# Polysketch attention and ELU experts on one core: batch 2's x from products of 64 rows, and a new order of the calls up to group 6

## The chip, the cores and the metric

The kernel runs on one core of one Trainium2 chip. The metric is device time in microseconds (us); less is better. A core has five engines that work side by side, each in the order of its own queue: TensorE (PE in the profile; its weight loads are PEld), VectorE (DVE), ScalarE (ACT), GpSimd (POOL) and SyncE (SP), which in this kernel only issues transfers. TensorE writes into PSUM, a memory of eight banks; the other engines read it from there. All other tiles lie in SBUF, a memory of 128 partitions.

## The reference

The program computes an attention block and feeds its output to an expert block with the ELU activation.

```python
# B, H, S, D = 4, 4, 1088, 32;  r = 8;  all float32
def phi(x):                       # 8 x 8 = 64 features
    a = einsum('rd,bhsd->bhsr', S1, x)
    b = einsum('rd,bhsd->bhsr', S2, x)
    return einsum('bhsi,bhsj->bhsij', a, b).reshape(B, H, S, 64)
q_p, k_p = phi(q), phi(k)
kv  = einsum('bhsf,bhsd->bhfd', k_p, v)      # 64 x 32 per head
z   = sum(k_p, axis=2)
num = einsum('bhsf,bhfd->bhsd', q_p, kv)
den = einsum('bhsf,bhf->bhs', q_p, z)[..., None] + 1e-6
x   = (num / den).transpose(0, 2, 1, 3).reshape(4352, 128)
h   = x @ w_in                               # 128 x 2048
g   = where(h > 0, h, exp(min(h, 0)) - 1)
out = g @ w_out                              # 2048 x 128
```

## The kernel before

**Tiles.** The 4352 tokens are cut into groups g = 0 to 8. Groups 0 and 1 are batch 0, 2 and 3 batch 1, 4 and 5 batch 2, 6 and 7 batch 3, each of 512 tokens; group 8 has the 64 tokens that are left over of each batch. The hidden width of 2048 is cut into eight pairs `cp` of 2 x 128 rows. One (g, cp) is called a step of the expert block here, and goes through the engines thus:

- `mm1(g, cp)` (line 910), TensorE: h = W_in x, two halves of 128 x 512, each into a PSUM bank of its own; four banks carry the tag "h" and are used in turn.
- `elu_a` (line 923), ScalarE: relu(-h) on line 930 and the exponential on line 932, giving e; `elu_d` (line 934), VectorE: gg = max(e - 1, h) on line 938. After it the bank is free for the next tenant.
- `sums7` (line 791), GpSimd: three sums of quarters of gg. `mm2_seven` (line 819), TensorE: W_out gg as seven products of half size (Strassen's way), which needs these sums. Group 0, and the first pair of group 1, use plain products instead (`mm2`, `mm2_blocks`).
- At the end of a group `fin_seven_copy`, `fin_seven_a`, `fin_seven_b` (lines 843 to 889; ScalarE, then VectorE) put the seven products together from the two banks "o0" and "o1", and `fin_seven_c` (line 890) transposes the result on VectorE and issues 16 stores on SP's queue (line 901).

**The queries.** The x of a group comes from its query features and the kv of its batch. `queries(g5s, g1s, step)` (line 751) takes two of the h banks, under the name of a step of the expert block, and two of the tag "aux". It makes two kinds of products into them: for groups in `g1s` the sketches of the queries (`q1`, line 567; products of 32 rows), for groups in `g5s` x itself. Between the two, VectorE makes the query features of a group: `q1_out` (copies to SBUF), `q2_prod`, `q2_sum`, `q2_rec`, `q2_an` (the denominator and the division by it), `q2_half` (the outer product, in two halves i; `q2_a` puts one factor into PSUM first), and `q4(g, i)` (line 702), which turns them so that the features lie on partitions.

x is made in one of two ways, by the tuple `pairs` on line 330. A group that isn't in it takes `q5` (line 719): the 64 features are summed in two products of 32 rows, f = 0 and 1, and `q4` is one VectorE transpose (line 707). A group in `pairs` takes `q5_pairs` (line 731): one product of 64 rows. For this the two feature halves of a head must lie in neighbouring blocks of 32 partitions, and `q4` has to move them there: a VectorE transpose (line 711), then eight transfers between partitions on SP's queue (line 717) for each half i, from the tile qpF to the tile raw or qpE. An entry g of `pairs` covers g and g + 1, as one `queries` call does. Before, these are groups 6 and 7 (batch 3) and group 8; groups 2, 3 (batch 1) and 4, 5 (batch 2) take `q5`.

**kv.** `KA(b)` (line 446) makes kv of batch b on TensorE. `KT_out(b)` (line 458) transposes it, stores it in DRAM (line 462, SP) and reads it back in the form that the products need, also on SP: four loads into `kvs[b]` (line 465) for `q5`, four or two loads into `kv2[b]` (line 469) for `q5_pairs`.

**Batch 0** starts the kernel and has helpers of its own (`KF_first`, `KO_first`, `KA_first`, `q1_first`, `q4_early`, `q5_early`, `den_turn`, `den_out` and others); its x comes from `q5_early_out` (lines 670 to 679) and starts the expert block through `mm1_first`. `q4_early` transposes query features on TensorE, four transposes a call. `transp` (line 284) transposes q or k on VectorE.

**Weights.** w_in and w_out arrive as 64-bit floats in words of 32 bits. `R1(f, i)` runs one of the steps strip, floor, shift, round_s, low, whole (lines 117 to 145) on one slice i of them; they are spread over VectorE, ScalarE and GpSimd in the first 40 us. `weights7` sums quarters of W_out for `mm2_seven`.

**The order.** From line 1022 to line 1893 the calls stand in an order written out by hand: what is called first goes first into the queue of its engine, and the semaphores follow from the data and from the reuse of buffers. From `steps[32]` (group 6, pair 0) on, a loop (lines 1896 to 1921) issues the steps in turn. `width[0] = 64` (line 1622) lets the products of `mm1` and `mm2_seven` that are issued after it go in tiles of 64 columns.

Of the kernel before, what the change touches and what calls it, by code (L numbers as in the profile page):

```python
# [12 lines left out]
F32 = mybir.dt.float32  # L13
# [16 lines left out]
def kernel(  # L30
# [301 lines left out]
    pairs = (6, 8)  # L332
    pair_b = [g // 2 for g in pairs if g < 8]
    kvs = {b: const.tile([P, H, 2, D], F32, name=f"kvs{b}") for b in (1, 2)}
# [141 lines left out]
    def Z(b, ps, zl):  # L476

        quarters(ps[:, 96:128], SXh[:], zl[:], None if b else 64)
# [547 lines left out]
    KF_first((0, 1), (4, 0))  # L1026
    KF_first((1, 1))
    KF_first((2, 1))
    transp(kT, "k", 0, 5, KT)
    KF_first((5, 0), (3, 1))  # L1030
    KF_first((6, 0), (4, 1))
    KF_first_out(0)
    transp(kT, "k", 0, KT + 5, NT)
# [3 lines left out]
    KF_first_out(1)  # L1037
    KF_first_out(2, slice(1, 2))
    KF_first_out(2, slice(0, 1))
    transp(qT, "q", 0, 0, 8)  # L1040
    KO_first(5, 6)
    Z_first(0, 1, 2)
    q1_first(0, 1)
    Z_first(3, 4, 5)
    Z_first(6, 7, 8)
    q1_first(2, 3)
    KO_first(3, 5)
    KO_first(6, 9)
    make_Sxp()
    KO_pool(0, 3)  # L1050
    load_rest()
    zl = ZC(0, feats["z"])
    Z(0, feats["z"], zl)
    Z_out(0, feats["z"])
    q1_first_out()
    KA_first(range(0, 5), True, False)
    zq = q1z_first()
    q2_out(0, 0)
    q2_out(0, 1)
    transp(qT, "q", 0, 8, 13)  # L1060
    q4_early(0, 0)
    KA_first(range(5, 9), False, True)
    q4_early(0, 1)
    q2_prod(0, zq)
    R1(strip, 0, nc.scalar)
    R1(low, 0)
    R1(strip, 1, nc.scalar)
    q4_out(0, 0)
    transp(qT, "q", 0, 13, NT)
    abwp = q1_second()  # L1070
    q2_sum(0)
    R1(floor, 0)
    KS_copy()
    KS_turn()
    q2_rec(0)
    den_wide()
# [4 lines left out]
    R1(shift, 0)  # L1081
    R1(shift, 1)
    q4_out(0, 1)
    R1(strip, 2, nc.scalar)
    den_out()
    R1(round_s, 1)
    q5_early(0)
    q2_prod(1)
    R1(low, 1, nc.gpsimd)
    R1(round_s, 0)  # L1090
    whole_half(0, 0)
    q2_sum(1)
    q5_early_out(0, 0)
    R1(low, 2)
    R1(low, 3)
    R1(low, 4)
    R1(strip, 3, nc.scalar)
    q5_early_out(0, 1)
    mm1_first(0, (0,))
    mm1_first(0, (1,))  # L1100
    elu_a(0, 0, 0, (0,))
    R1(strip, 4)
    q2_rec(1)
    R1(floor, 4)
    q2_an(1)
    R1(shift, 4)
    whole_half(0, 1)
    R1(whole, 1)
    mm1_first(1, (0, 1))
    elu_a(0, 0, 0, (1,))  # L1110
    q2_out(1, 1)
    mm1(0, 1, (1,))
    mm1(0, 1, (0,))
    q4_early(1, 1)
    R1(round_s, 4)
    q2_out(1, 0)
    elu_d(0, 0, 0)
    elu_a(0, 0, 1, (0,))
    q4_early(1, 0)
    elu_a(0, 0, 1, (1,))  # L1120
    elu_a(0, 1, 1, (0,))
    elu_a(0, 1, 1, (1,))
    elu_d(0, 0, 1)
    R1(whole, 4)
    mm1(0, 2, (0,))
    mm1(0, 2, (1,))
    R1(floor, 2)
    R1(shift, 2)
    R1(round_s, 2)
    q4_out(1, 1)  # L1130
    q4_out(1, 0)
    R1(strip, 7)
    elu_d(0, 1, 1)
    KT_out(0)
    elu_a(0, 1, 0, (0,))
    R1(floor, 3)
    R1(strip, 5)
    R1(whole, 2)
    elu_a(0, 2, 1, (0,))
    elu_a(0, 1, 0, (1,))  # L1140
    q5_early(1)
    q5_early_out(1, 1)
    q5_early_out(1, 0)
    mm2(0, 0, False, (0,))
    R1(shift, 3)
    R1(floor, 5)
    R1(low, 5)
    R1(round_s, 3)
    elu_a(0, 2, 1, (1,))
    R1(shift, 5)  # L1150
    R1(whole, 3)
    weights7(slice(1, 2), 0)
    mm2(0, 0, False, (1,))
    elu_a(0, 2, 0, (0,))
    elu_a(0, 2, 0, (1,))
    elu_d(0, 1, 0)
    R1(floor, 7)
    mm1(1, 0, (1,))
    mm1(1, 1, (0,))
    elu_d(0, 2, 1)  # L1160
    mm1(1, 0, (0,))
    R1(round_s, 5)
    elu_a(1, 1, 0, (0,))
    elu_a(1, 1, 0, (1,))
    R1(strip, 6)
    elu_d(0, 2, 0)
    R1(strip, 8)
    R1(floor, 6)
    R1(shift, 6)
    R1(floor, 8)  # L1170
    R1(round_s, 6)
    R1(whole, 5)
    elu_a(1, 0, 0, (0,))
    elu_a(1, 0, 0, (1,))
    R1(low, 6)
    elu_a(1, 0, 1, (0,))
    R1(shift, 7)
    mm2(0, 1, False, (0,))
    elu_a(1, 0, 1, (1,))
    R1(low, 7)  # L1180
    elu_d(1, 0, 0)
    mm2(0, 1, False, (1,))
    mm2(0, 2, False, (0,))
    mm2(0, 2, False, (1,))
    transp(kT, "k", 1, 9, NT)
    R1(shift, 8)
    R1(round_s, 7)
    mm1(1, 1, (1,))
    elu_a(1, 1, 1, (0,))
    elu_a(1, 1, 1, (1,))  # L1190
    R1(low, 8)
    transp(kT, "k", 1, 0, 9)
    elu_d(1, 0, 1)
    R1(whole, 6)
    mm2_blocks(0, (0,))
    mm1(0, 3, (0,))
    R1(low, 9)
    elu_d(1, 1, 1)
    R1(strip, 9)
    elu_d(1, 1, 0)  # L1200
    KF_late(1, None)
    R1(strip, 10)
    R1(round_s, 8)
    elu_a(0, 3, 0, (0,))
    elu_a(0, 3, 0, (1,))
    elu_d(0, 3, 0)
    R1(whole, 7)
    mm1(0, 3, (1,))
    elu_a(0, 3, 1, (0,))
    mm1(0, 4, (1,))  # L1210
    mm2_blocks(0, (1,))
    elu_a(0, 3, 1, (1,))
    mm1(0, 4, (0,))
    elu_a(0, 4, 0, (0,))
    elu_d(0, 3, 1)
    elu_a(0, 4, 0, (1,))
    KF_late_out(1, 1)
    weights7(slice(2, 4), 0)
    make_SWs()
    R1(floor, 10)  # L1220
    R1(floor, 9)
    R1(shift, 10)
    elu_d(0, 4, 0)
    R1(shift, 9)
    transp(kT, "k", 2, 0, 9)
    R1(round_s, 9)
    mm2(0, 3, False, (0,))
    mm2(0, 3, False, (1,))
    R1(whole, 8)
    mm1(0, 5, (0,))  # L1230
    mm1(1, 2, (1,))
    mm1(0, 5, (1,))
    R1(whole, 9)
    elu_a(0, 4, 1, (0,))
    elu_a(0, 4, 1, (1,))
    elu_d(0, 4, 1)
    KF_late_out(1, 0)
    elu_a(0, 5, 0, (0,))
    KO(1, 0, nc.gpsimd)
    mm2(0, 4, False, (0,))  # L1240
    mm2(0, 4, False, (1,))
    elu_a(0, 5, 1, (0,))
    elu_a(0, 5, 1, (1,))
    elu_d(0, 5, 1)
    elu_a(0, 5, 0, (1,))
    elu_d(0, 5, 0)
    KO_a(1, 1)
    KO_b(1, 1)
    R1(round_s, 10)
    transp(qT, "q", 1, 0, 9)  # L1250
    mm1(0, 6, (0,))
    R1(low, 10)
    R1(whole, 10)
    elu_a(0, 6, 0, (0,))
    mm1(1, 2, (0,))
    mm2(0, 5, False, (0,))
    elu_a(0, 6, 0, (1,))
    elu_a(1, 2, 1, (0,))
    elu_a(1, 2, 1, (1,))
    elu_a(1, 2, 0, (0,))  # L1260
    elu_a(1, 2, 0, (1,))
    KA(1, (0,))
    weights7(slice(1, 2), 1)
    KA(1, (1,))
    mm1(0, 6, (1,))
    transp(qT, "q", 1, 9, NT)
    KT_out(1)
    elu_d(0, 6, 0)
    weights7(slice(0, 1), 2)
    weights7(slice(2, 4), 1)  # L1270
    mm2(0, 5, False, (1,))
    zls[1] = ZC(1, kv_ps[1])
    sums7(1, 1, 0)
    Z(1, kv_ps[1], zls[1])
    elu_a(0, 6, 1, (0,))
    elu_a(0, 6, 1, (1,))
    elu_d(1, 2, 1)
    Z_out(1, kv_ps[1])
    Z_share(1)
    elu_d(0, 6, 1)  # L1280
    elu_d(1, 2, 0)
    sums7(1, 2, 0)
    weights7(slice(1, 2), 2)
    mm1(0, 7, (0,))
    elu_a(0, 7, 0, (0,))
    elu_a(0, 7, 0, (1,))
    mm2(0, 6, False, (0,))
    mm2(0, 6, False, (1,))
    mm1(0, 7, (1,))
    transp(kT, "k", 3, 0, 9)  # L1290
    elu_a(0, 7, 1, (0,))
    elu_d(0, 7, 0)
    sums7(1, 1, 1)
    weights7(slice(0, 1), 0)
    weights7(slice(1, 2), 3)
    sums7(1, 1, 2)
    transp(kT, "k", 3, 9, NT)
    queries((), (2,), (1, 4))
    mm1(1, 3, (0,))
    q1_out(2, (2,))  # L1300
    mm2(0, 7, True, (0,))
    q1_out(2, (1,))
    weights7(slice(4, 8), 0)
    elu_a(0, 7, 1, (1,))
    elu_d(0, 7, 1)
    q1_out(2, (3,))
    mm2(0, 7, True, (1,))
    mm1(1, 4, (1,))
    q1_out(2, (0,))
    q2_prod(2)  # L1310
    elu_a(1, 3, 0, (0,))
    elu_a(1, 3, 0, (1,))
    mm1(1, 3, (1,))
    elu_a(1, 3, 1, (0,))
    elu_d(1, 3, 0)
    fin1(0)
    q2_sum(2)
    sums7(1, 2, 1)
    weights7(slice(4, 8), 2)
    q2_rec(2)  # L1320
    elu_a(1, 4, 1, (0,))
    q2_an(2)
    mm1(1, 6, (1,))
    mm1(1, 4, (0,))
    elu_a(1, 3, 1, (1,))
# [648 lines left out]
```

## Time and profile before

| What | Value |
|---|---|
| median of 3 runs | 260.21 us (259.96 to 260.28) |
| the profiled execution, its own time | 260.24 us |
| its span | 258.3 us |
| granted TensorE clock, mean | 1.00 |
| longest busy on other engines: GpSimd, ScalarE, VectorE | 183.9, 182.1, 175.6 us |

The page gives one profiled execution. "Busy" is the time in which an engine executes, the percentage its share of the span. The page's table of the costliest groups shows which work this is and how the engines wait:

```profile
L938 DVE SCALAR_TENSOR_TENSOR gg<-e,h 128x512 f32<-128x512 f32 x128 | 85.4, 683 | 59.7 <-ACT e L932 42.2
L259 PE MATMUL h<-xg,W 128*32 128x512 f32 (+2 forms) x768 | 121.5, 584 | 0.7 <-DVE xg L678 0.7
L930 ACT ACTIVATE e<-h 128x512 f32<-128x512 f32 x128 | 75.0, 591 | 52.4 <-PE h L259 50.4
L795 POOL TENSOR_TENSOR tt<-gg 128x512 f32<-128x512 f32 x55 | 71.6, 1301 | 26.6 <-DVE gg L938 21.1
```

A row reads: line, engine, operation, the tile written and the tiles read, count; busy time in us and mean ns of one; then the idle time of the engine just before these instructions, and what ended most of it. ScalarE idles 52.4 us in front of line 930, and TensorE's h ends 50.4 us of that: ScalarE waits for TensorE.

### The profile page before, as it was taken

Reading aid. Unit: us, or ns where it says so; the run is one execution under the profiler, and the core shown is the slowest. Engines: PE = TensorE matmul, PEld = TensorE weight load, DVE = VectorE, ACT = ScalarE, POOL = GpSimd, SP = SyncE. Lnnn points to the kernel's source line nnn. Section 1 sums busy time; section 2 is a strip of 40 time slices with the busy share of each in tenths; the row PEclk is TensorE's granted clock in tenths of the full one; section 3 lists DMA queues with packets and bytes.
Section 4 is the critical chain, followed back from the end, with each engine's and each line's share of the span. In section 5 each row is a group of like instructions: output and inputs, shape, how many; then the busy total and the mean of one; then the engine's idle time right before and its main releaser. Section 6 shows DMA issues by size and latency. Waiting matters only on the chain.

```text
span 258.3 us, 9815 instructions
## 1 busy us (share of the span) xinstructions
PE 251.9 (98%) x4133; PEld 160.0 (62%) x4133; DVE 175.6 (68%) x342; ACT 182.1 (70%) x357; POOL 183.9 (71%) x236
## 2 busy tenths in 40 slices
PE   8789999999999999999999999999999999999994
PEld 7643333426666677567566666666766666667994
DVE  5799998898859875789665678743455445644641
ACT  2589887748757657667687777578777777777792
POOL 5433365698994978875779877987888888888310
PEclk9999999999999999999999999999999999999999
DMA  6999692303000111100110004321021100110021
GB/s 187 288 348 248 203 279 59 93 20 52 14 5 4 22 26 27 24 5 5 25 18 3 3 1 95 86 43 28 12 30 25 20 3 0 22 24 3 3 32 31
DMA packets 30427, 15.61 MB, mean 60 GB/s; under 512 B 22544, under 2 KB 28048, under 8 KB 30384
## 3 DMA queue, kind: packets, MB, share of 16 engines
q1 hardware_dynamic: 29520, 14.22, 23.2%
q10 hardware_dynamic: 800, 0.71, 1.0%
q8 instruction: 32, 0.52, 0.8%
q14 instruction: 11, 0.09, 0.1%
q0 software_dynamic: 64, 0.07, 0.1%
HBM read 11.31 MB, written 2.36 MB: 53 GB/s over the span
## 4 chain that ended last, share of the span: by engine, by line
PE 95%; DMA 2%; issue 1%; ACTq 1%; DVE 0%; ACT 0%; DVEq 0%
PE h L259 46%; PE pb L839 18%; PE pa L839 15%; PE o L259 5%; PE ol L259 3%; DMA hd_q<-in_q_dram 2%; PE kv L453 1%; PE qtp L640 1%; PE h L574 1%; PE h L726 1%; PE pb L815 1%; PE xps L666 1%; PE kv L439 1%; PE kfps L366 1%; PE h L738 0%
## 5 line engine op out<-in xcount | busy, mean ns | idle before, releaser
L938 DVE SCALAR_TENSOR_TENSOR gg<-e,h 128x512 f32<-128x512 f32 x128 | 85.4, 683 | 59.7 <-ACT e L932 42.2
L259 PE MATMUL h<-xg,W 128*32 128x512 f32 (+2 forms) x768 | 121.5, 584 | 0.7 <-DVE xg L678 0.7
L930 ACT ACTIVATE e<-h 128x512 f32<-128x512 f32 x128 | 75.0, 591 | 52.4 <-PE h L259 50.4
L795 POOL TENSOR_TENSOR tt<-gg 128x512 f32<-128x512 f32 x55 | 71.6, 1301 | 26.6 <-DVE gg L938 21.1
L932 ACT ACTIVATE e<-e 128x512 f32<-128x512 f32 x128 | 79.0, 630 | 3.0
L259 PEld LDWEIGHTS h<-xg,W 128*32 128x32 f32 (+1 forms) x768 | 34.2, 119 | 44.4 <-issue 32.2
L800 POOL TENSOR_TENSOR tt<-tt,gg 128x256 f32<-128x256 f32 x55 | 41.7, 759 | 3.1
L802 POOL TENSOR_TENSOR tt<-gg,tt 128x256 f32<-128x256 f32 x55 | 40.7, 744 | 3.1
L839 PEld LDWEIGHTS pa<-gg,W 128*64 128x64 f32 (+1 forms) x528 | 25.8, 125 | 25.5 <-issue 25.2
L839 PE MATMUL pa<-gg,W 128*64 128x128 f32 (+1 forms) x528 | 32.4, 273 | 0.0
L839 PE MATMUL pb<-tt,SS 128*64 128x128 f32 (+1 forms) x472 | 29.5, 273 | 0.0
L145 POOL TENSOR_TENSOR W<-W,raw 128x256 uint32<-128x256 uint32 (+2 forms) x12 | 11.7, 978 | 20.0 <-DVE W L119 8.3
L839 PE MATMUL pa<-tt,SS 128*32 128x128 f32 (+1 forms) x404 | 25.3, 273 | 0.0
L839 PEld LDWEIGHTS pb<-tt,SS 128*64 128x64 f32 (+1 forms) x472 | 22.7, 127 | 0.0
L839 PE MATMUL pb<-gg,SS 128*64 128x128 f32 (+1 forms) x292 | 21.9, 273 | 0.0
L839 PE MATMUL pb<-tt,W 128*64 128x128 f32 (+1 forms) x292 | 21.9, 273 | 0.0
L839 PEld LDWEIGHTS pa<-tt,SS 128*32 128x32 f32 (+1 forms) x404 | 17.0, 120 | 0.0
L259 PE MATMUL o<-gg,W 128*32 128x512 f32 x128 | 15.3, 593 | 0.0
L839 PEld LDWEIGHTS pb<-gg,SS 128*64 128x64 f32 (+1 forms) x292 | 13.9, 124 | 0.0
L839 PEld LDWEIGHTS pb<-tt,W 128*64 128x64 f32 (+1 forms) x292 | 13.9, 124 | 0.0
L991 DVE SCALAR_TENSOR_TENSOR gg<-e,h 128x256 f32<-128x256 f32 x16 | 6.6, 418 | 6.4 <-PE h L259 3.2
L259 PEld LDWEIGHTS o<-gg,W 128*32 128x32 f32 x128 | 4.1, 110 | 9.3 <-issue 7.1
(181 smaller groups left out, 273.3 us busy)
## 6 DMA issues: line engine op xcount, KB each, us to landing
raw<-in_moe_w_in_dram SPq DMA_DIRECT2D x8, 256.0 KB, 6.0
raw<-in_moe_w_out_dram SPq DMA_DIRECT2D x8, 256.0 KB, 5.7
out_dram<-ob SPq DMA_DIRECT2D x112, 16.0 KB, 1.5
hd_k<-in_k_dram SPq DMA_DIRECT2D x3, 544.0 KB, 8.5
hd_q<-in_q_dram SPq DMA_DIRECT2D x3, 544.0 KB, 10.0
v<-in_v_dram SPq DMA_DIRECT2D x4, 288.0 KB, 10.0
raw<-qpF SPq DMA_DIRECT2D x16, 64.0 KB, 2.0
v<-in_v_dram SPq DMA_DIRECT2D x3, 256.0 KB, 10.0
```

The lines of the kernel that those rows point to most:

```text
L145: nc.gpsimd.tensor_tensor(dst.bitcast(U32), dst.bitcast(U32), words(raw)[0], op=ADD)
L259: nc.tensor.matmul(dst[c:c + tile], lhs[:, c:c + tile], rhs, skip_group_check=True, tile_position=(0, c), **kw)
L366: nc.tensor.matmul(ps[g2][32 * c:32 * c + 32, :32 * KT], Sxp[r].rearrange("p x c r -> p (x c r)"), kT[b][r, u * KT:u * KT + KT, 32 * w:32 ...
L439: nc.tensor.matmul(kv_ps[0][32 * h:32 * h + 32, :R * R], vt[0][:, (h * KT + i) * D:(h * KT + i + 1) * D], feats[0, i // 5][:, i % 5, h].re ...
L795: nc.gpsimd.tensor_tensor(_ap(ts[g, cp][:, 0], [[4 * P, 2], [P, 2], [1, P]]), _ap(gs[g, cp][:, 0, P:], [[4 * P, 2]] + us), _ap(gs[g, cp][: ...
L800: nc.gpsimd.tensor_tensor(t[:, 1], t[:, 2], quarter(g, cp, 0, 0), op=ADD)
L802: nc.gpsimd.tensor_tensor(t[:, 3], quarter(g, cp, 1, 0), t[:, 1], op=SUB)
L839: nc.tensor.matmul(bank[r:r + width[0], P * col:P * col + P], lhs[:, w:w + width[0]], rhs[:, u], start=(first and i in ((0,) if g == 1 els ...
L930: nc.scalar.activation(e, hs[g, cp][c][:, :n], RELU, scale=-1.0)
L932: nc.scalar.activation(e, e, EXP, scale=-1.0)
L938: nc.vector.scalar_tensor_tensor(gs[g, cp][:, c, :n], es[g, cp][:, c, :n], -1.0, hs[g, cp][c][:, :n], op0=ADD, op1=MAX)
L991: nc.vector.scalar_tensor_tensor(gs["last", k // 2][:, k % 2, :2 * P], es["last", k // 2][:, k % 2, :2 * P], -1.0, hs["last", k][:, :2 * P ...
```

## The change

Four things differ; everything else in the file is the same.

1. `pairs` has 4 as well, so that groups 4 and 5 take `q5_pairs`, and `q4(4, 0)` and `q4(4, 1)` move their halves between partitions by the eight transfers of line 717. `kvs` is kept for batch 1 alone; so `KT_out(2)` issues no loads on line 465 where it issued four, and four on line 469 where it issued two.
2. The query products of groups 4, 5 and 8 are issued under the name of step (2, 7) instead of (3, 1): the banks that they take are those of an earlier step.
3. The calls from line 1025 to line 1893 are put into another order. They are the same calls with the same arguments, but for the step name of point 2.
4. `width[0] = 64` stands ahead of `mm1(3, 6, ...)` as before, but the query products of group 6 and x of group 4 now stand behind that `mm1`.

```diff
@@ -329,9 +329,9 @@
     kvS = const.tile([P, H, D], F32, name="kvS")
-    pairs = (6, 8)
+    pairs = (4, 6, 8)
     pair_b = [g // 2 for g in pairs if g < 8]
-    kvs = {b: const.tile([P, H, 2, D], F32, name=f"kvs{b}") for b in (1, 2)}
+    kvs = {b: const.tile([P, H, 2, D], F32, name=f"kvs{b}") for b in (1, )}
     kv2 = {b: const.tile([P, H, D], F32, name=f"kvp{b}") for b in range(B)}
```

With 872 calls in a new order the rest of the diff is long. The places that matter below are these. First the transposes of batch 0, with `mm1(0, 1, (0,))` between the two calls now:

```diff
     mm1(0, 1, (1,))
+    elu_a(0, 1, 1, (0,))
+    elu_a(0, 0, 1, (1,))
+    elu_d(0, 0, 0)
+    q4_early(1, 1)
     mm1(0, 1, (0,))
-    q4_early(1, 1)
...
+    R1(whole, 2)
     q4_early(1, 0)
```

In the first 16 us, the transpose of the last query tiles and one shift of weights stand ahead of the transposes on which the denominator waits; `transp(qT, "q", 0, 13, NT)` came behind `q4_out(0, 0)` before:

```diff
+    R1(floor, 0)
+    transp(qT, "q", 0, 13, NT)
+    KA_first(range(5, 9), False, True)
+    KS_copy()
+    R1(low, 0)
+    R1(shift, 0)
+    transp(qT, "q", 0, 8, 13)
     zq = q1z_first()
...
+    q2_prod(0, zq)
```

`KA(3)` is one call behind the other now, `KT_out(2)` and `KT_out(3)` both stand ahead of `fin_seven_c(1)`, and the query products of group 4 stand ahead of the last `mm1` of group 2:

```diff
+    KA(3, (0,))
+    KA(3, (1,))
...
+    fin_seven_c(1)
...
+    mm2_seven(2, 4, False, False)
+    queries((), (4, 8), (2, 7))
+    elu_a(2, 6, 1, (1,))
...
     mm1(2, 6, (0,))
-    KA(3, (0,))
...
-    mm1(3, 0, (0,))
-    KA(3, (1,))
...
-    queries((), (4, 8), (3, 1))
```

From there the new order up to x of group 4, the added lines alone, with most of `elu_a`, `elu_d` and `sums7` left out:

```diff
+    q1_out(4, (1,))
+    mm1(3, 0, (0,))
...
+    mm1(2, 7, (1,))
...
+    mm1(2, 7, (0,))
...
+    q2_prod(4)
...
+    q2_sum(4)
...
+    q2_rec(4)
...
+    q2_an(4)
...
     mm1(3, 2, (1,))
+    mm1(3, 1, (0,))
+    mm1(3, 1, (1,))
...
+    mm2_seven(2, 6, False, False)
+    q2_a(4, 1)
+    q2_half(4, 1)
...
+    q4(4, 1)
     mm1(3, 2, (0,))
...
+    q2_a(4, 0)
+    q2_half(4, 0)
...
+    fin_seven_copy(2)
...
+    mm1(3, 4, (0,))
+    mm1(3, 3, (0,))
...
+    mm1(3, 3, (1,))
+    fin_seven_a(2, 0)
+    fin_seven_b(2, 0)
...
     elu_d(3, 2, 0)
+    q4(4, 0)
+    mm2_seven(3, 0, True, False)
...
+    mm1(3, 4, (1,))
+    mm1(3, 5, (1,))
...
+    mm2_seven(3, 1, False, False)
+    mm1(3, 5, (0,))
...
+    mm2_seven(3, 2, False, False)
...
+    width[0] = 64
+    fin_seven_c(2)
...
     mm1(3, 6, (1,))
     mm1(3, 6, (0,))
+    sums7(3, 3, 2)
+    queries((4,), (6,), (3, 7))
```

## The prediction

> **What bounds the kernel now.** The profiled execution took 260.24 us by its own clock, 0.03 us over the median of the three runs (260.21); its span is 258.3 us, so 1.94 us lie around the span, and I change only the span. I read the page's busy table and its chain first, then who TensorE waited for, then the stretches by time.
>
> ```profile
> PE 251.9 (98%) x4133; PEld 160.0 (62%) x4133; DVE 175.6 (68%) x342; ACT 182.1 (70%) x357; POOL 183.9 (71%) x236
> ...
> PE 95%; DMA 2%; issue 1%; ACTq 1%; DVE 0%; ACT 0%; DVEq 0%
> ```
> ```profile
> PE h L259 <- DVE xg L678: 0.7, 1, 0.7
> ```
> ```profile
> 0.00:16.10 16.10, 13.19 (x220) 10.50 (x220) 11.30 (x39) 7.90 (x21) 7.56 (x27) 1.00 0.87 251
> 16.10:106.00 89.90, 89.90 (x1834) 47.06 (x1838) 74.46 (x140) 66.07 (x126) 63.55 (x86) 1.00 0.36 91
> ```
>
> The chain is TensorE for 95% of the span. Its last wait on another engine (0.7 us, for batch 0's x) ends at 16.1 us; in the stretch after that 89.90 of 89.90 us are busy, at a granted clock of 1.00, and the stretches up to 252 us are equally full. As ends of matmuls are modelled, I also went by starts: half a mm1 or mm2 step starts 0.858 us after the one before, a mm2_seven takes 1.53, and what is over these nominal distances sums to 1.2 us, always 0.08 to 0.16 where the tile shape changes. So from 16.1 us on there is no stall that a new order could remove. A gain must come from less TensorE work or from an earlier 16.1; a loss from any stall that the new order makes.
>
> **The products of group 4's x.** Before, `q5` made 32 products of 32 rows (two records each), beside group 6's query products; after, `q5_pairs` makes 16 of 64 rows. The prices are start-to-start in TensorE's order of time: products of 32 rows alone (group 2), of 64 rows (group 6, up to group 8's first), of both kinds in group 4's step, and query products alone (group 2):
>
> ```profile
> 70.02 0.40 PE L726 MATMUL h<-qpT,kvs 32*32 32x256 f32 x2
> ...
> 71.45 0.43 PE L839 MATMUL pa<-gg,W 128*32 128x128 f32 x8
> ```
> ```profile
> 122.11 0.41 PE L726 MATMUL h<-qpT,kvs 32*32 32x256 f32 x2
> ...
> 124.17 0.65 PE L259 MATMUL h<-xg,W 128*64 128x512 f32 x2
> ```
> ```profile
> 176.24 0.40 PE L738 MATMUL h<-raw,kvp 64*32 64x256 f32 x1
> ...
> 177.12 0.22 PE L738 MATMUL h<-qpE,kvp 64*32 64x64 f32 x1
> ```
> ```profile
> 52.81 0.40 PE L574 MATMUL h<-qT,SWs 32*32 32x256 f32 x2
> ...
> 53.47 1.07 PE L259 MATMUL h<-xg,W 128*32 128x512 f32 x8
> ```
>
> Group 2 alone took 1.43 us, the 64-row products 0.88, group 4's step 2.06, query products alone 0.66. After: 0.88 + 0.66 = 1.54 for 2.06, a saving of 0.52 us. Between the two kinds the tile shape now changes inside the step: 0 to 0.15 us by the changes above, I take 0.05. [...]
>
> **What feeds them.** `q4(4, i)` keeps one VectorE transpose (1.23 us now on L711, 1.24 on L707: nothing) but adds eight copies between partitions on SP's queue for each half, 16 in all; `KT_out(2)` loses its four loads of kvs and gains two of kv2, 7 issues to 5. The copies of groups 6 and 8 show the price: eight issues took 4.97 us (0.62 each), landing 2.0 us after issue. SP is never TensorE's releaser, but these copies now gate the step. Ahead of them on SP stand `KT_out(2)`, `KT_out(3)` and the 16 stores of group 1 (9.66 us now). Both KT_outs are emitted before the stores, earlier than now; by my count of the queue the stores end near 106 us and the first q4 is ready near 110. Behind the copies stand only group 2's stores, for which no engine waits soon.
> The deadline, counted in TensorE work from the end of `queries((), (4, 8), (2, 7))`: the step of group 4 comes 16 half steps of 0.858 and 6 mm2_sevens of 1.53, 22.9 us, later. VectorE's work up to the end of `q4(4, 0)` is 15.3 us; 4.3 to the last issue and 2.0 to land make 21.6. Margin 1.3 us; so it costs nothing on the path, and all lateness beyond 1.3 if this cover goes.
>
> **The order.** The calls are the same 872 but for one step number. For each TensorE instruction I counted the TensorE work of the new order between it and what it needs, against the queued work of the engine that makes it. From an h tile's last product to the next tenant of its bank the shortest distance is 3.09 us (2.64 before); relu, exp and gg need 0.59 + 0.63 + 0.69 = 1.9. From a step's last mm1 to its mm2_seven it is 5.5 us (6.2 before), against 4.7 unqueued (these 1.9 and POOL's 1.3 + 0.75 + 0.74), and the last sum is read 1.3 us into the mm2_seven. Group 2 to 3 hands over the o banks in 2.57 us (1.71 at the shortest before). None is over its limit, so I take 0 for stalls behind the first us; the tightest are the rivals below.
> Two things in the order do have a price. Batch 0's second set of eight transposes (`q4_early(1, 1)` and `(1, 0)`) was one block; now `mm1(0, 1, (0,))` stands between. Entry and exit cost 0.14 and 0.15 us (8 transposes took 1.02 of 0.88 nominal, and the mm1 ahead 0.14 too much), so +0.29; batch 3's `KA` becomes one block for two, -0.08. Together +0.21.
> The first stretch: TensorE runs from the landing of v at 10.03 through the same products, in another order, to the end of den_turn at 14.70 now; the sum of the pieces is equal. But VectorE makes `transp(qT, "q", 0, 13, NT)` and a shift (0.37 + 0.20) between the landing at 11.21 and the transpose that the den chain needs, and copies the second half of qpT 0.7 later, with 0.2 + 0.3 + 0.34 + 0.25 of other work before xg. I get xg at 15.6 for 15.53. Bounds: 0.15 earlier (ScalarE, not TensorE, holds den_out by that) to 0.5 later; I take +0.1.
>
> **Sum.** 260.24 - 0.52 + 0.05 + 0.21 + 0.10 = 260.08 by the profiled execution, 260.1 rounded, and the 0.03 us to the median do not show in it. 0.2% (0.52 us) is about what a measurement of this kernel can tell from no change.
>
> **Rivals.**
> (1) VectorE is late in group 4 (slower). The transposes, products and q4 of group 4 now all stand between the query products and group 2's hand-over. From those queries to `elu_d(3, 2, 1)`, which frees the bank of `mm1(3, 4, (0,))`, VectorE has q1_out 1.84, pw 0.44 to 0.99, den 0.49, reciprocal 0.39, an 0.55, five gg at 0.60, two q2_half at 1.13, a q4 at 1.25: 10.2 to 10.8 us, in 8 x 0.858 + 3 x 1.53 = 11.45 us of TensorE work. For: now VectorE idles 3.1 us of the 20 in this region on ScalarE and TensorE; two thirds of it in the new stretch, 2.1 us, make it 0.8 to 1.4 late. Against: ScalarE's exps stand ahead of each gg by my count. It decides beyond 0.65 to 1.25 us of waiting; with such waits and the same again at the hand-over the time is 260.1 + 1.2 = 261.3. Chance 0.21.
> (2) The copies land late: an issue of 1.54 us, the longest of these 16, in place of 0.62 in each half, or landings of 3.5 us (the slowest), use up the 1.3 and 1 us more: 261.1. Chance 0.06.
> (3) The first 16 us of the order have margins of 0.3 to 0.7 (`q5_early(1)`, `whole(6)` for `mm1(0, 3, (0,))`) where before the nearest had 0.8 to 1.2; POOL and VectorE hold each other up there (a W sum 1.08 us for 0.82). Two such misses: 260.6 to 261. Chance 0.10, half of it within the 0.2%.
> (4) Nothing is saved by 64 rows, the step keeping its 2.06: 260.1 + 0.47 = 260.6. Against it stands the row of 0.88. Chance 0.03.
> (5) The start comes 0.15 earlier instead of 0.10 later, and the transposes, split, drain at no cost: 260.1 - 0.25 - 0.21 to 0.29 = 259.5 to 259.6. For it: only 1.2 us lie over the nominal distances in the whole run, so most tile changes cost far less than these. Chance 0.20.
>
> **How the numbers follow.** The forecast, 259.7 to 260.4, has 0.40. Faster by over 0.2% is (5) and a little of the forecast's edge, 0.22; slower (1), (2) and half of (3), 0.32; the rest, 0.46, within. The range goes from (5) to (1): 259.5 to 261.3.
>
> **What would show it.** Right: TensorE's stretch from 16.1 to 252 us full as now; L738 with 32 more records and L726 with 64 fewer; group 4's step 1.5 to 1.6 us long; the two blocks of transposes at 18.9 and 20.5 us apart, each with 0.1 to 0.15 over its nominal time; xg at 15.5 to 15.7. (1) shows as TensorE idle behind gg or cc near 112 to 116 us, (2) as a wait of L738 for a DMA near 124, (3) as idle between 20 and 33 us. Wrong would be a single stall over 0.5 us after 33 us at a place not named here.

## The result and the profile after

The changed kernel took 261.35 us (median of 12 runs, 261.07 to 264.12) against 260.02 for the kernel before on the same chip (12 runs): a ratio of 1.0073, interval 1.0054 to 1.0092. By the medians it is 1.33 us slower; the ratio, which is of the fast runs alone, makes 1.9 us of it (1.4 to 2.4), and the account below is of the 1.33. Predicted was 260.1, in a range of 259.5 to 261.3; the time lies just outside. The profiled execution took 261.17 us, with a span of 259.1.

First the busy table and the shares of the chain, then the two stretches that the prediction showed (us, busy time and instructions of TensorE, its weight loads, VectorE, ScalarE, GpSimd, then the granted clock, the DMA share and GB/s), then what TensorE waited for; all of the changed kernel:

```profile
PE 252.5 (97%) x4101; PEld 158.9 (61%) x4101; DVE 174.4 (67%) x342; ACT 180.8 (70%) x357; POOL 184.7 (71%) x236
...
PE 94%; POOL 2%; DVE 1%; issue 1%; ACT 0%; DVEq 0%
```
```profile
0.00:16.10 16.10, 13.85 (x235) 11.00 (x239) 12.31 (x43) 8.86 (x23) 8.39 (x28) 1.00 0.85 254
16.10:106.00 89.90, 89.19 (x1801) 45.41 (x1794) 74.61 (x144) 63.14 (x121) 61.47 (x81) 1.00 0.35 90
```
```profile
PE h L259 <- DVE xg L678: 0.7, 1, 0.7
PE pb L839 <- issue: 0.5, 1, 0.5
...
PE pb L839 <- POOL SS L786: 0.2, 1, 0.2
```

TensorE has the 32 products fewer that were meant (4101 for 4133), but the stretch from 16.1 to 106 us is no longer full: 89.19 of 89.90. Two waits of mm2_seven (L839) are new. Busy time hides a part of them, because the ends of matmuls are modelled; so the account below goes by starts, as the prediction's did. "Start" is from the first product of batch 0's kv to the first mm1, "main" from there to TensorE's last record; kv is when the first product of kv began.

| us | before | after | after less before |
|---|---|---|---|
| kv | 10.03 | 9.33 | not counted |
| start | 6.07 | 5.95 | -0.12 |
| main | 238.46 | 239.91 | +1.45 |
| start + main | 244.53 | 245.86 | +1.33 |

The sum equals the difference of the medians; what makes the ratio larger, no profile here shows. kv is left out because it varies from one execution to the next: in a second profile of the unchanged kernel (below) kv began at 9.00 us, with start and main again 6.07 and 238.46. The wait ahead of kv in the first profile (0.81 us, "issue") was gone there, so it belongs to the execution and not to the kernel. It fits a late landing of v: its transfers took 10.0 us at the median in the first profile and 9.1 in the second.

The +1.45 of the main part has five places, found by laying TensorE's starts beside each other. A stand is a stretch in which TensorE starts nothing, less the usual distance. There are stands of 0.14 at 65.8 us, 0.38 at 68.4 us and 0.81 at 89.6 us; +0.28 for the two blocks of transposes; -0.16 for the step of group 4's x. 0.14 + 0.38 + 0.81 + 0.28 - 0.16 = 1.45.

**The stands at 65.8 and 68.4 us.** GpSimd's rows in order of time (start, us, engine, line, tiles, count, and in brackets the idle time before), and TensorE's; both of the changed kernel:

```profile
62.15 2.21 POOL L795 TENSOR_TENSOR tt<-gg 128x512 f32<-128x512 f32 x1 [4.32 <-DVE gg L938]
64.43 0.75 POOL L800 TENSOR_TENSOR tt<-tt,gg 128x256 f32<-128x256 f32 x1
65.26 0.74 POOL L802 TENSOR_TENSOR tt<-gg,tt 128x256 f32<-128x256 f32 x1
65.95 1.29 POOL L795 TENSOR_TENSOR tt<-gg 128x512 f32<-128x512 f32 x1
67.32 0.74 POOL L800 TENSOR_TENSOR tt<-tt,gg 128x256 f32<-128x256 f32 x1
68.02 0.73 POOL L786 TENSOR_TENSOR SS<-W,SS 128x256 f32<-128x256 f32 x1
```
```profile
61.99 1.22 DVE L699 TENSOR_TENSOR qp<-an,abw 128x1024 f32<-128x1024 f32 x1
```
```profile
68.23 0.40 PE L839 MATMUL pb<-gg,W 128*32 128x128 f32 x8
68.80 0.32 PE L839 MATMUL pb<-gg,SS 128*32 128x128 f32 x4 [0.17 <-POOL SS L786]
```

The sum of (1, 3) took 2.21 us, the same sum of (1, 4), at 65.95, 1.29: while the first ran, VectorE (second fence) multiplied two SBUF tiles for 1.22 us. So the chain of sums ends 0.92 late. The product behind the stand at 65.8 begins at 66.05; the sum that it reads (L802) ends at 66.00. And the last weight sum (L786), the fourth call of `weights7` for W_out's rows 4 to 7, stands behind it in GpSimd's queue and ends at 68.7, after the products that came before its reader had been issued. The sum of (1, 3) and the product of VectorE overlap from 62.15 to 63.21, 1.06 us, and GpSimd lost 0.92. Beside products of the same shape with one factor in PSUM (L699, qp<-qa,abw) sums of this size took 1.27 to 1.29 us: four in the kernel before, at overlaps of 0.84 to 1.14 us, and one in the changed kernel, at 1.17. The experiment e7 puts the two cases to the test.

This slowing is not new with the change. The kernel before has it at the same sum, GpSimd's row and then VectorE's, both of the kernel before:

```profile
60.43 2.20 POOL L795 TENSOR_TENSOR tt<-gg 128x512 f32<-128x512 f32 x1 [0.66 <-DVE gg L938]
```
```profile
60.27 1.22 DVE L699 TENSOR_TENSOR qp<-an,abw 128x1024 f32<-128x1024 f32 x1
```

It cost TensorE nothing there: the sum began 4.70 us ahead of the mm2_seven that reads it (65.13), against 2.45 in the changed kernel (64.60), and the weight sum ended at 65.11, ahead of the mm2_seven at 68.38 that needs it. So the new order starts both late, and the old slowing on top of that makes the stands.

**The stand at 89.6 us** has no engine named. TensorE's rows in order of time, of the changed kernel:

```profile
88.31 0.63 PE L839 MATMUL pa<-gg,W 128*32 128x128 f32 x15
...
89.62 0.27 PE L839 MATMUL pb<-tt,W 128*32 128x128 f32 x1
90.43 0.31 PE L839 MATMUL pb<-tt,W 128*32 128x128 f32 x4 [0.54 <-issue]
```

Seven of eight products of one kind come 0.81 us after the first; the sum that they read, made by GpSimd, was ready at 89.43 us, and the first product, at 89.62, had it. "issue" means that the profile shows nothing that held the engine. The experiments point to the loading of its instructions.

### The profile page after: what moved, and what is told of

Read it like the earlier page. It is cut to its first block, busy times and chain, and to the rows that moved or that the text cites. A ratio compares the mean times of both kernels' runs of the same rounds, so it can differ in the third digit from the quotient of the medians.

```text
span 259.1 us, 9778 instructions
## 1 busy us (share of the span) xinstructions
PE 252.5 (97%) x4101; PEld 158.9 (61%) x4101; DVE 174.4 (67%) x342; ACT 180.8 (70%) x357; POOL 184.7 (71%) x236
## 4 chain that ended last, share of the span: by engine, by line
PE 94%; POOL 2%; DVE 1%; issue 1%; ACT 0%; DVEq 0%
PE h L259 44%; PE pb L839 17%; PE pa L839 14%; PE o L259 5%; PE ol L259 3%; PE idle L267 1%; POOL tt L795 1%; PE kv L453 1%; PE qtp L640 1%; PE h L738 1%; DVE gg L938 1%; PE h L574 1%; PE pb L815 1%; POOL tt L800 1%; PE abp L346 1%
## 5 line engine op out<-in xcount | busy, mean ns | idle before, releaser
L259 PE MATMUL h<-xg,W 128*32 128x512 f32 (+2 forms) x768 | 119.9, 584 | 0.7 <-DVE xg L678 0.7
L802 POOL TENSOR_TENSOR tt<-gg,tt 128x256 f32<-128x256 f32 x55 | 40.6, 742 | 3.5
L800 POOL TENSOR_TENSOR tt<-tt,gg 128x256 f32<-128x256 f32 x55 | 40.7, 741 | 3.3
L839 PEld LDWEIGHTS pa<-gg,W 128*64 128x64 f32 (+1 forms) x528 | 25.6, 125 | 22.5 <-issue 22.1
L839 PE MATMUL pa<-gg,W 128*64 128x128 f32 (+1 forms) x528 | 32.7, 273 | 0.0
L839 PE MATMUL pb<-tt,SS 128*64 128x128 f32 (+1 forms) x472 | 29.7, 273 | 0.0
L839 PE MATMUL pa<-tt,SS 128*32 128x128 f32 (+1 forms) x404 | 25.5, 273 | 0.0
L839 PEld LDWEIGHTS pb<-tt,SS 128*64 128x64 f32 (+1 forms) x472 | 22.9, 127 | 0.0
L839 PE MATMUL pb<-tt,W 128*64 128x128 f32 (+1 forms) x292 | 22.3, 273 | 0.5 <-issue 0.5
L839 PE MATMUL pb<-gg,SS 128*64 128x128 f32 (+1 forms) x292 | 22.1, 273 | 0.2 <-POOL SS L786 0.2
L839 PEld LDWEIGHTS pa<-tt,SS 128*32 128x32 f32 (+1 forms) x404 | 17.2, 120 | 0.0
L839 PEld LDWEIGHTS pb<-tt,W 128*64 128x64 f32 (+1 forms) x292 | 14.0, 124 | 1.0 <-issue 0.8
L839 PEld LDWEIGHTS pb<-gg,SS 128*64 128x64 f32 (+1 forms) x292 | 14.0, 124 | 0.4 <-POOL SS L786 0.4
L259 PE MATMUL h<-xgl,W 128*64 128x128 f32 x128 | 9.4, 273 | 0.0
```

Source lines behind the costliest of these rows:

```text
L259: nc.tensor.matmul(dst[c:c + tile], lhs[:, c:c + tile], rhs, skip_group_check=True, tile_position=(0, c), **kw)
L800: nc.gpsimd.tensor_tensor(t[:, 1], t[:, 2], quarter(g, cp, 0, 0), op=ADD)
L802: nc.gpsimd.tensor_tensor(t[:, 3], quarter(g, cp, 1, 0), t[:, 1], op=SUB)
L839: nc.tensor.matmul(bank[r:r + width[0], P * col:P * col + P], lhs[:, w:w + width[0]], rhs[:, u], start=(first and i in ((0,) if g == 1 els ...
```

## The experiments

All times are medians; the ratio is to the kernel before, on the same chip. Start and main as above, kv in the last column; they are of one profiled execution each. The runs were made on several chips, so times of different runs are compared by their ratios, or by main.

| run | us | ratio, interval | start | main | kv |
|---|---|---|---|---|---|
| e1_shift | 262.82 | 1.0107, 1.0087 to 1.0127 | 7.43 | 239.33 | 9.79 |
| e2_weights | 260.94 | 1.0042, 1.0026 to 1.0058 | 5.95 | 239.51 | 9.07 |
| e3_old_x | 261.61 | 1.0055, 1.0035 to 1.0076 | 5.95 | 240.25 | 9.57 |
| e4_pairs_alone | 268.18 | 1.0331, 1.0297 to 1.0366 | 6.07 | 248.51 | 9.21 |
| e5_shift56 | 261.5 | 1.0052, 1.0025 to 1.0078 | 5.95 | 239.10 | 10.11 |
| e6_mended | 261.06 | 1.0049, 1.0028 to 1.007 | 5.95 | 238.27 | 11.0 |
| e7_q2a | 262.12 | 1.0101, 1.0046 to 1.0156 | 7.46 | 240.48 | 10.29 |
| e8_ka_earlier | 262.11 | 1.0089, 1.0057 to 1.0122 | 5.94 | 240.57 | 10.59 |
| e9_mended2 | 260.48 | 1.003, 1.0009 to 1.0051 | 6.86 | 238.26 | 9.26 |
| e10_mended3 | 260.72 | 1.0039, 1.0018 to 1.006 | 6.95 | 238.58 | 8.91 |
| e11_join | 261.49 | 1.006, 1.004 to 1.0079 | 5.95 | 239.89 | 9.43 |
| e12_before_again | 259.20 (one run) | | 6.07 | 238.46 | 9.00 |
| e13_fewer | 260.71 | 1.0051, 1.0033 to 1.0069 | 5.95 | 239.32 | 9.37 |
| e14_mended4 | 259.99 | 1.0011, 0.9992 to 1.003 | 5.95 | 238.79 | 9.25 |

All but e4 and e12 are edits of the changed kernel.

**e1_shift: other instructions ahead.** `keep_warm` issues products at the start whose result nobody reads; more of them move the whole sequence by 116 instructions and leave the rest as it is.

```diff
-    keep_warm(3)
+    keep_warm(8, 192, 32)
```

> The changed kernel with 32 short warm-up matmuls (8 x 4 of 192 columns) in the first 3 us in place of 3 long ones: 29 matmuls, 116 TensorE instructions, more, the order of everything else untouched. Theory A, loading of instructions: the 0.81 us in which TensorE stands in the last product of mm2_seven(2, 0) (89.62 to 90.43 us) is a wait for the next 256 instructions, since KA(3) in one block uses up 180 of them in 1.2 us; moving the 256-boundaries by 116 spreads the block over two loads, the stand shrinks to under 0.2 us and the time falls by 0.6 to 0.8 us to about 260.6. Theory B, a wait for the sums of GpSimd or another engine: nothing changes, the stand stays at 0.8 us and the time at 261.3.

The stand at 90 us was gone (main 0.58 less), as by theory A, but the time rose to 262.82 where 260.6 was expected. A new stand of 1.4 us came at 11.1 us, among batch 0's query products (start 7.43 for 5.95); the waits of TensorE in e1:

```profile
PE zqp L540 <- issue: 1.2, 1, 1.2
```

Nothing of the data or of another engine near 90 us was changed, so neither made the stand. It moved with the count of instructions.

**e2_weights: the weight sum a place earlier.**

```diff
     weights7(slice(4, 8), 1)
+    weights7(slice(4, 8), 3)
...
-    weights7(slice(4, 8), 3)
```

> The changed kernel with weights7(slice(4, 8), 3) moved up to behind weights7(slice(4, 8), 1), into the 4.3 us in which GpSimd idles before sums7(1, 3, 0). Theory A: the stand of 0.38 us in mm2_seven(1, 4) at 68.4 us is the wait for this sum, which stands behind four late sums; it goes, the 0.14 us at 65.8 stays, and the time falls by 0.3 to 0.4 us to about 260.9. Theory B, the late gg of (1, 3) itself holds mm2_seven(1, 4): the stand only moves to its later products, and the time stays within 0.1 us.

Main 0.40 less: the stand of 0.38 at 68.4 us is gone, and the one near 90 stays (0.80). So moving this one call takes the 0.38 away, though the sum of (1, 3) took 2.21 as before.

**e3_old_x: the new order with the old products for batch 2.**

```diff
-    pairs = (4, 6, 8)
+    pairs = (6, 8)
...
-    kvs = {... for b in (1, )}
+    kvs = {... for b in (1, 2)}
```

> The changed kernel's order and step names with pairs = (6, 8) and kvs of batch 2 as before: x of group 4 by products of 32 rows, no copies. By my prediction the step gets 0.47 us longer (2.06 for 1.54 to 1.59), 261.8. By the trace of the changed kernel the step and the tile changes around it took 2.06 us (0.15 + 1.75 + 0.05 + 0.11) against 2.22 before; the products of 32 rows would cost 2.22 plus the change to tiles of 64 columns ahead of them, so 0.2 to 0.3 us more, 261.55. If the copies on SP hurt something that the trace does not show as TensorE idle, the time falls below 261.3.

Main 0.34 more than the changed kernel's, of which 0.04 lie in the stand near 90: within the new order the products of 64 rows gain, and the order, not they, makes the loss. The ratios alone (1.0055 and 1.0073) do not tell the two apart.

**e4_pairs_alone: the new products in the old order** (the same two lines of the kernel before, set as in the change).

> The kernel before, in its own order, with pairs = (4, 6, 8) and kvs for batch 1 alone. q4(4, 0) ended at 121.1 us with the step at 122.1; eight issues take 4.3 to 5.0 us to the last and 2.0 to land. Theory A: TensorE waits 5 to 6 us for the copies at the step, the work of the other engines hides none of it, less 0.5 for the products: 264.5 to 266. Rival: the wait is shorter, since q4(4, 0) is emitted last and VectorE has room to run ahead, or the stall lets late engines catch up: 261 to 263.

8.2 us slower by the medians, 10.05 by start and main of the profiled execution, which took 269.64 us, 1.46 over its median. The waits of TensorE, and four stretches, both of e4:

```profile
PE h L738 <- DMA raw<-qpF: 4.0, 1, 4.0
```
```profile
106.00:120.70 14.70, 14.70 (x348) 9.74 (x344) 13.44 (x25) 10.79 (x21) 11.49 (x14) 1.00 0.15 32
120.70:125.30 4.60, 0.65 (x8) 0.00 (x0) 2.27 (x4) 1.23 (x2) 1.75 (x2) 0.99 0.35 78
125.30:135.70 10.40, 9.66 (x76) 2.54 (x78) 1.86 (x5) 1.25 (x3) 4.23 (x6) 0.51 0.31 56
135.70:150.00 14.30, 14.30 (x174) 9.79 (x172) 7.03 (x14) 11.02 (x21) 8.35 (x9) 1.00 0.02 3
```

TensorE stood 4.0 us for the copies between partitions, and then the granted clock was 0.51 for 10.4 us. By starts against the kernel before, the first product of x came 4.07 us late; group 4's step took 6.03 us for 2.06, 3.97 more, with two more waits for copies in it (0.26 and 0.35 us); the mm1 behind it lost another 2.01 at the low clock. 4.07 + 3.97 + 2.01 = 10.05. The forecast, 264.5 to 266, had the wait but not the clock. So in the old order the copies cost far more than the products save; in the new one, with q4 earlier, no product waited for them. In this trace the clock was low from 125.24 to 135.48 us, 10.24 us; the two later waits end at 126.64 and 129.20, and behind them TensorE worked for another 6.28 us at the low clock. What sets its length, no run shows.

**e5_shift56 and e6_mended: a shift of 56 instructions, alone and with three repairs.**

```diff
-    keep_warm(3)
+    keep_warm(1)
+    keep_warm(4, tile=32)
```

> The changed kernel with 14 more warm-up matmuls (1 long and 16 short ones for 3 long ones, 56 TensorE instructions more), nothing else. In the run with 116 more, the stand at 89.6 us was gone, and a new one of 1.4 us stood behind KA_first, at the 450th instruction; the two stand at places 2816 = 11 x 256 instructions apart. Theory A, instructions loaded 256 at a time: with 56 more neither block of KA products lies ahead of a boundary; both stands are gone, first mm1 to last product takes 239.1 us (239.91 in the changed kernel), the time is 260.5. Theory B, the first shift only moved other waits about: a stand of 0.5 us or more remains at one of the two places.

e6 adds e2's edit, joins the transposes again and sets the tile width after the query products instead of before the mm1 ahead of them:

```diff
-    q4_early(1, 1)
     mm1(0, 1, (0,))
+    q4_early(1, 1)
...
-    width[0] = 64
     queries((4,), (6,), (3, 7))
+    width[0] = 64
```

> The changed kernel with four edits: the 56 instructions more of the run above, weights7(slice(4, 8), 3) early, mm1(0, 1, (0,)) ahead of q4_early(1, 1) so that the eight transposes are one block, and width[0] = 64 behind the queries of groups 4 and 6. Theory: the terms add up, -0.81 - 0.38 - 0.28 - 0.11 = -1.58 from first mm1 to last product (238.3 for 239.91; 238.46 in the kernel before), and the time is 259.6 to 259.9, within 0.2% of before or just faster. Rival: the work that was late in a stand is late elsewhere without it (POOL's sums near 66 us, the copies for x of group 4 with 0.3 to 0.8 us to spare); then 0.3 to 1 us comes back as a new stand, 260.2 to 260.8.

In both the stand near 90 us is gone, and no other came: main 239.10 and 238.27, as theory A and the sum of the terms had it, the latter 0.19 under the kernel before. But the times, 261.5 and 261.06, missed 260.5 and 259.6 to 259.9. The new warm-up is longer (5.00 and 5.81 us, for 3.65): the first products of k began at 6.23 and 7.13 us instead of 5.21, and kv with them. What the main part gained the first 11 us took back.

**e7_q2a: VectorE's other factor from PSUM.** `q2_a(2, i)` ahead of each `q2_half(2, i)`, as groups 4 to 7 have it.

> The changed kernel with q2_a(2, i) ahead of both q2_half(2, i), so that VectorE reads one factor from PSUM as it does in groups 4 and 6; 0.26 us more on ScalarE each. Theory A: the sum of 2.21 us at 62.15 (1.29 elsewhere) is slowed by VectorE's q2_half at 61.99 with both factors in SBUF; it takes 1.3 us, GpSimd's chain comes 0.9 us earlier, and both stands at 65.8 (0.14) and 68.4 us (0.38) are gone: 260.8. Theory B: the sums are late because gg of (1, 3) is late; the stands stay, 261.3 or a little more for the copies on ScalarE.

GpSimd's first sum, then VectorE's product in the same region, both of e7:

```profile
65.84 1.29 POOL L795 TENSOR_TENSOR tt<-gg 128x512 f32<-128x512 f32 x1 [5.55 <-DVE gg L938]
```
```profile
66.06 1.22 DVE L699 TENSOR_TENSOR qp<-qa,abw 128x1024 f32<-128x1024 f32 x1 [0.30 <-ACT qa L692]
```

The two run side by side, from 66.06 to 67.13, and the sum takes 1.29, not 2.21; the product takes 1.22 in both cases. The rest of theory A did not come, and the time, 262.12, missed both forecasts. VectorE now waits for ScalarE's copies and gg comes later: the sum begins only 1.38 us ahead of its mm2_seven (67.22), for 2.45. In this execution all of it lies 2.5 us later than in the changed kernel (first mm1 at 17.75 for 15.27), 1.5 of it because the granted clock was 0.51 from 10.29 to 13.72 us (start 7.46). The stand on the weight sum is gone, but that of 0.14 has become 0.29 (at 68.4), and a wait of 0.86 for gg and its bank is new (at 69.5): a cure that costs more than the harm.

**e8_ka_earlier: kv of batch 3 half a step earlier.** `mm1(2, 3, (0,))` moved behind `KA(3, (1,))`, which gives GpSimd's sum for mm2_seven(2, 0) more time.

> The changed kernel with mm1(2, 3, (0,)) behind both halves of KA(3) in place of ahead of them, so that 32 instructions of 0.86 us stand between the 180 of KA(3) and mm2_seven(2, 0). Theory A (loading of instructions): the stand of 0.81 us is gone or under 0.2 us, and unless KA(3) now waits for its features, first mm1 to last product takes 239.1 to 239.3 us, the time 260.5 to 260.7. Theory B (sums of GpSimd): the sum that mm2_seven(2, 0) reads is ready at the same time as before, the stand stays.

The sum was then ready 0.6 us before its use (90.83 for 91.44), and the stand came at the same instruction all the same (0.78 us). The theory that the sums of mm2_seven(2, 0) are late is refuted. But theory A's forecast, a stand under 0.2 us and 260.5 to 260.7, was missed too: the load of instructions (next paragraph) came later as well, at 89.49 us with 102 instructions to go to the stand, for 87.85 and 165 in the changed kernel. `KA` itself now waited for its bank, 0.77 us from the product ahead of it.

**What the stands share.** Count all of TensorE's records in their order: products, weight loads and 63 semaphore and drain instructions of its own. The ten stands that no wait for data explains all come behind a number that leaves 193 when divided by 256: 3265 in the changed kernel, e2, e3, e7, e8 and e11; 449 in e1, e9 and e10; 3777 in e14. (For the one in e7 the profile names a sum, but one that this mm2_seven does not read.) The page's table of DMA queues of the changed kernel has a row that fits:

```profile
q8 instruction: 32, 0.52, 0.8%
```

32 transfers of 16 KB, for 4101 products, as many weight loads and the 63 others: 8265 = 32 x 256 + 73. (e13, with 168 products and weight loads fewer, has 31 transfers.) In all 16 traces the number of transfers is that of the full 256s. So one transfer is read here as one load of 256 of TensorE's instructions; no row names their engine. One of them starts at 87.85, and the first instruction after the stand at 90.43: 2.58 us. In e1 it is 9.97 to 12.54, 2.57; over the stands 2.2 to 2.7.

The traces allow a sharper test than the stands alone. Let the n-th load belong to number 193 + n x 256: the 12th to 3265, the first to 449. That gives 494 pairs in the 16 traces. In none did TensorE go on behind that number less than 2.19 us after the load's start. In 13 it did so within 2.8 us, and all ten stands are among these; the other three went on without a stand, and so did the later ones, but for a gap of 0.16 us at 2.83. In the kernel before the shortest is 3.68, 3.46 in its second profile. So by this reading the stands come where TensorE arrives before the load can serve it.

The same stretch of time, in the changed kernel and in the kernel before, shows how fast instructions went meanwhile:

```profile
87.85:89.62 1.77, 1.77 (x98) 1.77 (x88) 0.34 (x2) 1.77 (x5) 1.69 (x4) 1.00 0.06 9
```
```profile
87.85:89.62 1.77, 1.77 (x33) 0.73 (x28) 1.77 (x3) 0.88 (x3) 1.64 (x3) 1.00 0.08 18
```

186 products and weight loads against 61. At the start of the 12th load TensorE had 165 instructions to go to number 3265 in the changed kernel, 296 in the kernel before. `KA(3)`, now one block (90 products and 90 weight loads in 1.22 us), stands directly before a mm2_seven (56 and 56 in 1.53 us): by this reading TensorE uses up what it has before the next piece is there. In the kernel before half a step of mm1 (16 instructions in 0.86 us) stood between the halves of `KA`. What sets the start of a load, no run shows.

**e9_mended2 and e10_mended3: a shorter warm-up, and one more reordering.** e9 is e6 with `keep_warm(4, 128, 32)`; e10 is e9 with `elu_d(1, 3, 0)` ahead of `elu_d(1, 4, 1)`, so that GpSimd begins its sum before VectorE's long product.

> The four edits of the mended run once more, with the 16 short warm-up matmuls cut to 128 columns, since those of 256 made the first products of k start at 6.2 and 7.1 us in place of 5.2. First mm1 to last product 238.3 us as there (238.46 in the kernel before, 239.91 in the changed one); first products of k at 5.2 us again, so the start is 5.95 us behind the first product of kv as in the changed kernel (6.07 before). Theory: the time is 259.6 to 259.9 us, ratio to before 0.998 to 1.000. Rival, that the changed start is worse in a way that one profile does not show: over 260.3 though the trace is full.

> The run above with elu_d(1, 3, 0) ahead of elu_d(1, 4, 1) on VectorE, so that GpSimd's sum of (1, 3) starts 0.6 us earlier. Theory: the stand of 0.14 us near 66 us, which is left there, goes (238.15 us from first mm1 to last product, 259.5 to 259.8). Rival: gg of (1, 4) comes 0.6 us later, frees its bank later, and mm1(1, 5, (1,)) or mm1(1, 6, (1,)) waits 0.1 to 0.5 us: 238.3 to 238.7.

Both times, 260.48 and 260.72, missed 259.6 to 259.9 and 259.5 to 259.8. In e9 the main part keeps 238.26 and kv is back at 9.26, but the stand fell into the first stretch, at number 449, where the dense products of batch 0's queries are; the waits of TensorE in e9:

```profile
PE abwp L550 <- issue: 0.7, 1, 0.7
```

By starts it cost 0.91, the start's 6.86 for 5.95. In e10 the sum began 0.6 us earlier against its mm2_seven and the stand of 0.14 went, but the release of a bank came later, as the rival had it: a new stand of 0.44 us at 66.9, main 238.58.

**e11_join: the transposes in one block again** (e6's second edit alone).

> The changed kernel with mm1(0, 1, (0,)) ahead of q4_early(1, 1), so that the eight transposes are one block again. By the prediction's own price (0.14 us for entry and 0.14 for exit of a block) first mm1 to last product falls by 0.28 us to 239.6 and the time to 261.05. Rival: the copies behind the transposes come later and q5_early(1) waits for them; no gain.

The block lost its extra 0.28, and main stayed (239.89 for 239.91), but not for the rival's reason: what came 0.28 earlier to the stand waited nearly as much longer there (1.08 for 0.81). The load of instructions had hardly come earlier with it: 72.48 us behind the first mm1, for 72.58.

**e12_before_again**: the kernel before, profiled once more; its reading stands at the top, under the result.

> The kernel before, unchanged, for a second profile. In the first, TensorE's products of kv began at 10.03 us, 1.12 us behind the product ahead of them; with its order in the run with pairs alone at 9.21, 0.24 behind. If the landing of v differs from run to run, first mm1 stands 6.07 us behind the first product of kv again and 238.46 us ahead of the last product, with the start itself anywhere from 15.2 to 16.2. If the late start belongs to this kernel, it is 16.1 again.

**e13_fewer: fewer instructions where they are dense.** Products of 64 columns for the two steps before `KA(3)`, 168 instructions fewer.

```diff
+    width[0] = 64
     mm1(2, 0, (1,))
...
+    width[0] = 32
     KA(2, (0,))
```

> The changed kernel with tiles of 64 columns from mm1(2, 0, (1,)) to mm1(2, 4, (0,)), the same products in half as many instructions, 168 fewer ahead of KA(3); order and start untouched. Theory A (instructions are loaded 256 at a time): the boundary that stood in mm2_seven(2, 0) falls 168 instructions later, beyond the block, and the stand of 0.81 us goes; the change of tile shape ahead of KA(2) costs 0.1 us. First mm1 to last product 239.15 to 239.3 (239.91), the start 5.95 us behind the first product of kv, the time 260.6. Theory B (something else in mm2_seven(2, 0)): the stand stays at 0.7 to 1.1 us, 261.3.

The place of the stand, TensorE's rows of e13:

```profile
89.34 0.66 PE L839 MATMUL pb<-tt,SS 128*32 128x128 f32 x16
89.78 0.44 PE L839 MATMUL pb<-tt,W 128*32 128x128 f32 x8
90.00 0.26 PE L259 MATMUL kv<-zl,SXh 128*32 128x32 f32 x5
```

The eight products go in one run, 0.22 us to what follows, as theory A had it. The loads of instructions began at 85.43, ahead of `KA(3)`, and at 89.43 us; in the changed kernel at 82.63 and in the midst of `KA(3)`, at 87.85. Main 0.59 less; the 0.81 of the stand less two more changes of the tile form, which would be 0.11 each by the rest.

**e14_mended4: e13 with e2's edit, the joined transposes and the width behind the queries.**

> The run above with weights7(slice(4, 8), 3) early, the eight transposes as one block and width[0] = 64 behind the queries of groups 4 and 6. Theory: 239.2 - 0.38 - 0.28 - 0.11 = 238.4 from first mm1 to last product (238.46 in the kernel before), start 5.95 behind the first product of kv (6.07 there): within 0.2% of before, 259.6 to 259.9. If the time is over 260.3, something in the changed order costs time that TensorE's profile from first mm1 to last product does not show.

Main 238.79 for the 238.4 expected, with a small new stand (0.33 us at 100 us, number 3777). The interval, 0.9992 to 1.003, includes 1: the order mended thus is not told apart from the kernel before. No version here is shown to beat it.

## Why the prediction was wrong, point by point

- **"None is over its limit, so I take 0 for stalls behind the first us."** This step failed, by 1.33 us, in two ways. (a) GpSimd's chain was priced with 1.3 + 0.75 + 0.74 us, its undisturbed rows; beside VectorE's product the first took 2.21, as the profile of the kernel before already had it (2.20), and the place of the weight sum behind it was not followed at all. That cost 0.14 + 0.38: e2 shows the second, e7 the contention, and the 0.14 went in e10 with an earlier sum. (b) I counted for each instruction the data and banks that it needs, and not the instructions themselves: 0.81. e1, e5 and e13 show that this stand goes with the count, and e8 that it does not go with the data; that the load of 256 instructions is the mechanism rests on the numbers 193 + n x 256 and the times of the 494 loads.
- **The other terms** add up to nothing: -0.16 for group 4's x, +0.28 and -0.12 below. That the loss equals the stands so exactly is luck: the forecast had -0.16 for these terms, and its misses, +0.31 for group 4's x, +0.08 for `KA` and -0.22 for the start, nearly cancel.
- **The products of group 4's x, -0.47.** Measured -0.16. Before, the step with its changes of tile form took 0.113 + 2.056 + 0.05 = 2.22. After:

```profile
122.89 1.94 PE L259 MATMUL h<-xg,W 128*64 128x512 f32 x8
124.75 0.40 PE L738 MATMUL h<-raw,kvp 64*32 64x256 f32 x1
...
125.78 0.41 PE L574 MATMUL h<-qT,SWs 32*32 32x256 f32 x2
...
126.50 0.66 PE L839 MATMUL pa<-gg,W 128*64 128x128 f32 x8
```

  These are TensorE's rows of the changed kernel: 1.03 for L738 and 0.72 for L574, so 1.75 by starts for the 1.54 + 0.05 predicted: from the last L738, at 125.47, to the first L574 it is 0.31 us, and the change of tile form inside the step, taken at 0.05, cost 0.15, its upper bound. Then 0.112 (to 64 columns, at 122.9) and 0.15 (out of them into the step) come ahead, for 0.113 before, and 0.05 behind it: 1.75 + 0.112 + 0.15 + 0.05 = 2.06. That the mm1 ahead of the query products now goes in 64 columns was costed at nothing.
- **The transposes, +0.29**: measured 0.28. Right. **Batch 3's `KA` in one block, -0.08**: nothing. Its two parts took 1.59 us in the kernel before, without the half step between them, and the one block 1.59.
- **The start, +0.10**: measured -0.12. The bound of 0.15 earlier was nearer; half of rival (5).
- **The copies, hidden by a margin of 1.3 us**: held. 16 issues took 12.52 us (110.56 to 123.08), the second half of them 5.83, landing 2.0 to 2.6 us after issue; L738 began at 124.75 without waiting. The margin was 0.3 to 0.8 and not 1.3. Rival (2) did not happen, and e4 shows its price where the order gives no time.
- **Rival (1)**, VectorE late in group 4: no stand near 112 to 116 us. **Rival (3)**: none from 20 to 33. Its W sum of 1.08 us, in the kernel before at 18.82, ran beside VectorE's product of two SBUF tiles (L627); the sums of that size took 0.75 to 0.87 elsewhere. VectorE's L127, 0.82 us beside a W sum at 16.20, took 0.28 at 22.72 with none beside it. **Rival (4)**: e3 shows a gain of 0.30 to 0.34. That rival (1) had named 261.3 is a coincidence: none of its waits came. The forecast named in advance what would refute it, a single stall over 0.5 us after 33 us at a place not named; that is the 0.81 at 89.6 us.

## What to carry to other kernels

When an order is changed on an engine that is full, price each neighbour with the rows of what will run beside it, and follow every instruction of the slower queues, weight sums too: a slowing that costs nothing in the old order can cost in the new one, where its work starts closer to its use. Look also at how many instructions the bounding engine has per us: by the reading above, the blocks of small products put end to end here (186 products and weight loads in 1.77 us, for 61 in the kernel before) outran the loading of instructions, which no wait on data showed and which the shift of 116 in e1 only moved. Compare two kernels by starts between fixed points of work, not by one span each: the first product of kv alone varied by 1.03 us here between two profiles of one kernel.

## What the runs showed of the hardware

- The changed kernel had 32 transfers of 16 KB on the queue of instructions for 8265 records of TensorE, e13 31 with 168 fewer: in all 16 traces one for each full 256. From the start of such a load to the first instruction behind its number 2.2 to 2.7 us passed at the ten stands. The stands were 0.33 to 1.4 us long, all ten behind a number 193 + n x 256. In 494 loads of 16 traces TensorE never went on behind that number sooner than 2.19 us after the load's start. That the load is what they wait for is the reading that fits all ten; the profile has no row that says so.
- A GpSimd sum of 128x512 took 2.21 us beside a VectorE product of two SBUF tiles and 1.29 beside one with a factor in PSUM (e7). Both hold in the kernel before too (2.20, and 1.27 to 1.29).
- After 4.0 us without work the granted clock was 0.51 in the mean of a stretch of 10.4 us, with TensorE at work in that time but for two waits of 0.26 and 0.35 us (e4).
